# Batch 7's normalization factor through DRAM, batch 5's q transposed by DMA, and a new order, in a linear-attention and gated-FFN kernel

## The chip, the cores and the metric

The kernel runs on one core of a Trainium2 chip. The metric is the device time of one execution in microseconds (us). TensorE (PE; its weight loads are PEld) multiplies matrices into PSUM, VectorE (DVE) and ScalarE (ACT) work element by element, GpSimd (POOL) here issues the loads that cast from fp32 to bf16, and SyncE (SP) issues DMAs without a cast. Each engine runs its own instructions in program order and waits on semaphores for the others.

## What is computed

```python
def _attn_ref(q, k, v, g_norm):                    # q, k, v: (8, 8, 576, 64)
    kv = np.einsum('bhsd,bhse->bhde', k, v)
    out = np.einsum('bhsd,bhde->bhse', q, kv)
    rms = np.sqrt(np.mean(out * out, axis=-1, keepdims=True) + 1e-06)
    return (out / rms * g_norm).astype(np.float32)

def _moe_ref(x, w_in, conv_w, w_out):              # x: (8, 576, 512), d_ff 1024
    h = np.maximum(x @ w_in, 0.0)
    hp = ...                                       # h with one row of zeros at each end
    for k in range(3):
        conv_out += conv_w[k][None, None, :] * hp[:, k:k + S, :]
    gate = 1.0 / (1.0 + np.exp(-conv_out))
    return (h * gate @ w_out).astype(np.float32)
```

x is the attention's output with the heads side by side. The inputs are fp32; the products run in bf16.

## The kernel before

**Layout.** Between the two products everything is held transposed: features on the 128 partitions, the 576 positions of a batch along the free dimension. The 512 features of x are four tiles t of 128 (two heads each), the 1024 of h eight tiles f. Positions are halved into e = 0, 1 of 288 (HS) where a PSUM bank of 512 fp32 would be too small. Batches go in pairs p (0 to 3); x and h of a pair share a tile.

**The order is written out by hand.** ORDER (L66) is a list of tokens such as `sp.7.0@4,0`: the operation `sp` with arguments 7 and 0, and behind the @ the slots of ring buffers or PSUM banks that it takes, in turn. `:1` picks the other engine for operations that can run on ScalarE or VectorE. A loop (L732) calls the operations in this order, and L742 to L750 fix it on every engine. Between engines only data and buffers order the work, so a token's place matters against the tokens of its own engine.

**Stages of a batch b.**
- Loads: `Lq`, `Lk`, `Lv` (L299) through GpSimd's queue, one DMA of 590 KB in bf16 each (batch 1 in halves), into two slots a letter; `Li` and `Lo` load the weights. Batch 0 comes in `pre` (L215): q, k and v by pairs of heads through GpSimd's queue (L239), except the first k and v, which SP loads in fp32 into `stg` (L220) and `ca` (L326) casts on VectorE.
- `kv` (L356): k transposed times v, per head; `kvc`, or `kvn` with `ky` or `kx`, copy it to SBUF.
- q has to be transposed. Batches 0 to 4's way, `qt` or `qtp`, is TensorE (L378; for the batches in QP, 4 and 5, in the form of L386), and `qc` copies the result out of PSUM. For the batches in QD (6 and 7) `dq` (L434) has SP transpose q from SBUF to SBUF by DMA.
- q times kv: `ot` (L428, L429), or `oq` (L462) for the batches of QP and QD.
- `sq` (L491) squares on ScalarE, `oc` copies the product to `o32` in SBUF.
- The normalization. For batches 2 to 7, `ss` (L573) sums the squares of each head with the selector `sel`, so that a tile `ss` holds, for each t, rows of (batch in its group, e, head). NORM (L58) tells which batches share such a tile: group 3 is 6 and 7. `ln` (L582) takes the reciprocal root on ScalarE, `sl` (L589 to L592) splits the fp32 result into three bf16 parts on VectorE, `sp` (L601) spreads them over the 64 partitions of a head with a matmul against `spread`, which also adds the parts, and `mu` (L608) multiplies product, g_norm and factor on VectorE into xT. `ln` needs another table of ScalarE than the sigmoid (L211 loads tables).
- `hm` (L619): x times w_in, 8 matmuls a token; `re` (L625, L627) applies the relu into h.
- The convolution and the gate on five groups c (CONV, L63; groups 2 to 4 are pairs of batches): `ta` (L661, L662) the outer taps, `aa` (L668) and `ab` (L674) the sums, `sg` (L680) the sigmoid on ScalarE, `mg` (L686) the product with h.
- `om` (L696; `oh`, L711, for the last tile): h times w_out, by 128 positions m of pair p; `ea` or `eh` copies to a row tile, `st` or `sh` (L730, L725) stores it through SP.

**Fillers.** `unread.n` (L425) is n matmuls whose result nobody reads. 39 stand in the order of before, 10 of them ahead of the first q.

**Around the change.** SP's queue holds the two staged loads, then, from 63 us on, the stores, the four `dq` and four `kx` of batches 6 and 7. ScalarE's queue has the two small loads of g_norm and conv_w and the first table load at its head. qT, o32, row, k, v and the others are rings of slots by name. Which slots a load takes decides on whose last reader it waits.

Of the kernel before, what the change touches and what calls it, by code (L numbers as in the profile page):

```python
# [68 lines left out]
on.0.0@4 ot.0.1@2 qt0.0.2@6 nl.0.0@0 sq.0.1@1 unread.4@7 kv.0.2.1@7 on.0.1@4 qc0.0.2:1@1 al.x0@0 mu0.0.0 kvc.0.2.1.0
kvc.0.2.1.1:1 qt0.0.3@6 nl.0.1@1 ot.0.2@0 Li.0 unread.3@7 kv.0.3.1@7,4 mu0.0.1 sq.0.2@2 qc0.0.3:1 al.h0@0  # L70
kvc.0.3.1.0 on.0.2@2 kvc.0.3.1.1:1 ot.0.3@6 nl.0.2@2 sqh.0.3.0@3 Li.3 mu0.0.2 unread.3@5 onh.0.3.0@2 sqh.0.3.1
nlh.0.3.0@3 onh.0.3.1 Lq.1.2 nlh.0.3.1 qt.1.0@0 qc.1.0:1@2 Lv.1.2 unread.7@5 kv.1.0.2@0 muh.0.3.0 muh.0.3.1
kvc.1.0.2.0@1 kvc.1.0.2.1 unread.2@5 ot.1.1@0 sq.1.1@4 hm.0.0@6 on.1.1@2 hm.0.1@4 re.0.0 nl.1.1@4 ta.0.0@0 mu0.1.1
ot.1.0@6 hm.0.6@2 hm.0.7@0 Lk.1.2 re.0.1 sq.1.0@5 re.0.6 ta.0.1 aa.0.0 ta.0.6@1 on.1.0@2 qt.1.1@4 re.0.7 kv.1.2.2@0
nl.1.0@5 ab.0.0 qc.1.1@3 kvc.1.2.2.0 Li.1 kvc.1.2.2.1 ta.0.7 mu0.1.0 Lv.2.0@0 unread.3@1 ot.1.2@0 Li.2 Lk.2.0@0
ot.1.3@4 sq.1.2@6 unread.2@2 on.1.2@6 Lq.2.0@0 Lk.3.0@1 aa.0.3 sq.1.3@7 on.1.3@2 ab.0.3 nl.1.2@6 hm.0.3@6 nl.1.3@7
mu0.1.2 sg.0.0 hm.0.2@0 sg.0.1 re.0.2 mu0.1.3 hm.1.2@4 hm.0.5@2 sg.0.7 sg.0.6 re.0.3:1 Lv.3.0@1 pl mg.0.0 hm.1.3@6
hm.1.0@0 ta.0.2@0 al.x1@1 re.0.5 re.1.2 ta.0.3 re.1.0 mg.0.3 kv.2.0.4@2 aa.0.1 re.1.3 al.h1@1 ab.0.1 hm.1.1@4
ta.1.2@1 ta.1.3 hm.0.4@6 hm.1.7@0 aa.1.1 kvc.2.0.4.0@0 sg.0.2 sg.0.3 kvc.2.0.4.1 re.1.1 re.0.4 re.1.7 Lq.3.0@1
qt.2.0@2 qt.2.1@4 mg.0.1 hm.1.5@6 ab.1.1 ta.0.4@0 qc.2.0@4 Lo.0 sg.1.2 sg.1.3 ot.2.0@2 ta.0.5 hm.1.4@0 re.1.5  # L80
sq.2.0@0 qc.2.1@0 oc.2.0@0 mg.1.1 ot.2.2@4 ot.2.1@6 re.1.4:1 sq.2.2@1 kv.3.0.4@2 aa.0.2 oc.2.2@1 ot.2.3@0
kvc.3.0.4.0:1@1 sq.2.1@2 ab.0.2 ta.1.0@1 oc.2.1 sq.2.3@3 hm.1.6@4 ss.2@3 qt.3.1@6 re.1.6:1 sg.0.5 qt.3.0@4 oc.2.3
kvc.3.0.4.1:1 sg.0.4 qc.3.1@1 qc.3.0@2 ta.1.1 ln.8@0 unread.1@0 ot.3.3@6 unread.1@0 ot.3.0@4 Lo.1 ot.3.2@0 sq.3.0@4
mg.0.2 oc.3.0@2 Lq.4.0@0 aa.1.0 om.0.0.0@2 ta.1.4@0 sl.8@0 ta.1.5 ab.1.0 aa.1.2 sq.3.2@5 om.0.1.0@3 oc.3.2@3
om.0.2.0@4 sq.3.3@6 ot.3.1@0 om.0.0.4 oc.3.3 om.0.2.4 sq.3.1@7 oc.3.1 sp.2.0@6,0 ea.0.0@0 ss.3@5 ea.0.2@1 om.0.3.0@2
mu.2.0.0 ln.1@0 mu.2.0.1 sp.2.1@4,6 Lv.4.0@0 om.0.3.4 Lk.4.0@0 mu.2.1.0 qtp.4.0@0 sg.1.0 mu.2.1.1 sl.1@0 hm.2.6@4
qc.4.0:1@3 hm.2.2@6 re.2.6 ea.0.3@2 ab.1.2 re.2.2 sp.3.0@4,0 sg.1.4 sg.1.1 om.0.1.4 mu.3.0.1 mu.3.0.0 kv.4.0.4@2
sg.1.5 kvn.4.0.4 sp.3.1@0,6 ky.4.0.4.0 ea.0.1@3 hm.2.5@4 ky.4.0.4.1 re.2.5 mu.3.1.1 mu.3.1.0 hm.2.4@6 Lq.5.0@1
# [692 lines left out]
```

## Time and profile before

| what | us |
|---|---|
| median of 3 runs (180.3 to 180.98) | 180.41 |
| the profiled execution | 180.37 |
| its span, first to last instruction | 178.6 |
| first staged load issued (SP) | 0.75 |
| first matmul on data | 5.85 |
| last TensorE instruction | 174.45 |
| first table load of ScalarE | 2.37 |
| transposes of batch 6 and 7 by DMA issued | 86.3, 92.3, 94.6, 97.0 |

The granted TensorE clock is 0.996 of full speed over the span. The span starts with the first instruction and ends with the last; 1.8 us of the time lie around it. Busy time of TensorE includes the draining of a pipelined matmul: the cost of one in a row is the distance from its start to the next one's. The same holds, less strongly, for ScalarE and VectorE, whose instructions overlap by about 0.1 us. The DMA share is that of the 16 engines; above 1 it counts overlapping packets.

### The profile page before, as it was taken

The numbers are of one execution on the slowest core, as the hardware profiler recorded it, in microseconds if no ns is written. First come the engines' busy times: TensorE is split into PE (matmuls) and PEld (weight loads), VectorE is DVE, ScalarE is ACT, GpSimd is POOL, SyncE is SP. The second block draws the span as 40 slices with busy tenths as digits, with TensorE's granted clock in tenths as the row PEclk, the third lists the DMA queues.
The fourth block names the chain that finished last, engine by engine and source line by source line (L and its number), as shares of the span: only waits on it lengthen the run. The fifth ranks groups of instructions, "written<-read, shape, count | busy, mean of one in ns | idle before, by whom it ended". The sixth has DMA issues, their size and how long they took to land.

```text
span 178.6 us, 4103 instructions
## 1 busy us (share of the span) xinstructions
PE 170.6 (96%) x1680; PEld 101.0 (57%) x1680; DVE 140.4 (79%) x238; ACT 149.2 (84%) x235; POOL 30.6 (17%) x54
## 2 busy tenths in 40 slices
PE   6999997999999999999999999999999999999990
PEld 2434664787545677737657774344678744445450
DVE  5544199799999899999999999968999999930000
ACT  2479679999999999999999999999789986853341
POOL 7985528005320210600000000000000000000000
PEclk9999999999999999999999999999999999999998
DMA  5999999999999999999939700420340003046574
GB/s 150 193 183 197 200 201 202 204 205 204 205 204 204 204 207 251 175 188 193 153 99 228 207 4 0 165 101 32 136 158 0 4 0 117 0 185 225 186 259 149
DMA packets 32619, 27.58 MB, mean 154 GB/s; under 512 B 6080, under 2 KB 28120, under 8 KB 32600
## 3 DMA queue, kind: packets, MB, share of 16 engines
q0 software_dynamic: 21760, 15.96, 59.0%
q1 hardware_dynamic: 10800, 11.34, 20.3%
q8 instruction: 13, 0.21, 0.5%
q14 instruction: 6, 0.05, 0.1%
q10 hardware_dynamic: 40, 0.01, 0.0%
HBM read 32.52 MB, written 9.44 MB: 235 GB/s over the span
## 4 chain that ended last, share of the span: by engine, by line
PE 76%; ACT 10%; DVE 4%; DMA 3%; POOL 3%; issue 2%; POOLq 0%; ACTq 0%
PE bank L696 35%; PE bank L619 27%; ACT taps L680 3%; DMA q_sb<-in_q_dram 3%; ACT h L625 3%; PE bank L356 3%; PE bank L425 2%; PE bank L601 2%; PE bank L462 2%; PE bank L429 1%; PE bank L386 1%; POOL q_sb L239 1%; PE bank L573 1%; ACT o L339 1%; PE bank L711 1%
## 5 line engine op out<-in xcount | busy, mean ns | idle before, releaser
L619 PE MATMUL bank<-xT,w_in_sb 128*128 128x288 bf16 x512 | 66.3, 286 | 0.6 <-ACT root L540 0.6
L696 PE MATMUL bank<-w_out_sb,h 128*128 128x512 bf16 x280 | 64.3, 380 | 0.0
L619 PEld LDWEIGHTS <-w_in_sb 128*128 128x128 bf16 x512 | 49.1, 98 | 15.2 <-issue 1.7
L696 PEld LDWEIGHTS <-h 128*128 128x128 bf16 x280 | 26.1, 98 | 30.5 <-issue 1.2
L680 ACT ACTIVATE taps<-taps,cwn 128x1152 bf16<-128x1152 bf16 (+1 forms) x40 | 41.4, 1087 | 2.1 <-DVE taps L674 2.0
L625 ACT ACTIVATE h<-bank 128x576 bf16<-128x576 f32 x61 | 38.5, 680 | 2.4 <-PE bank L619 1.7
L339 ACT ACTIVATE row<-bank 128x512 f32<-128x512 f32 (+1 forms) x37 | 21.6, 604 | 11.6 <-PE bank L696 8.5
L686 DVE TENSOR_TENSOR h<-h,taps 128x2304 bf16<-128x2304 bf16 (+1 forms) x20 | 22.1, 1114 | 2.5 <-ACT taps L680 2.4
L668 DVE TENSOR_TENSOR taps<-taps 128x2304 bf16<-128x2304 bf16 (+1 forms) x20 | 22.3, 1119 | 0.4
L674 DVE TENSOR_TENSOR taps<-taps,h 128x2304 bf16<-128x2304 bf16 (+1 forms) x20 | 22.3, 1113 | 0.2
L661 DVE TENSOR_SCALAR taps<-h,cwn 128x1152 bf16<-128x1152 bf16 (+1 forms) x40 | 18.6, 465 | 4.3 <-ACT h L625 4.3
L491 ACT ACTIVATE sq<-bank 128x576 bf16<-128x576 f32 x28 | 19.1, 712 | 1.0 <-PE bank L429 1.0
L608 DVE SCALAR_TENSOR_TENSOR xT<-o,cw,bank 128x576 bf16<-128x576 f32 x24 | 18.2, 810 | 1.6 <-PE bank L601 1.5
L662 DVE TENSOR_SCALAR taps<-h,cwn 128x1152 bf16<-128x1152 bf16 (+1 forms) x40 | 18.2, 455 | 0.0
L339 ACT ACTIVATE o<-bank 128x576 f32<-128x576 f32 x24 | 16.9, 725 | 0.0
L425 PE MATMUL bank<-fill 128*128 128x512 bf16 x39 | 12.4, 445 | 1.5 <-DVE fill L226 1.5
L211 ACT ACT_TABLE_LOAD x8 | 10.3, 1283 | 2.5 <-issue 2.4
L356 PEld LDWEIGHTS <-k_sb 96*64 96x64 bf16 x384 | 7.3, 113 | 3.3 <-issue 3.1
L299 POOL DMA_DIRECT2D q_sb<-in_q_dram x8 | 6.0, 752 | 16.1 <-PE bank L378 14.3
L356 PE MATMUL bank<-v_sb,k_sb 96*64 96x64 bf16 x384 | 8.3, 197 | 0.2
L299 POOL DMA_DIRECT2D k_sb<-in_k_dram x8 | 6.1, 765 | 13.7 <-PE bank L356 13.1
L299 POOL DMA_DIRECT2D v_sb<-in_v_dram x8 | 6.0, 751 | 12.6 <-PE bank L601 11.4
(83 smaller groups left out, 122.8 us busy)
## 6 DMA issues: line engine op xcount, KB each, us to landing
out_dram<-row SPq DMA_DIRECT2D x35, 256.0 KB, 2.5
v_sb<-in_v_dram POOLq DMA_DIRECT2D x6, 576.0 KB, 13.8
k_sb<-in_k_dram POOLq DMA_DIRECT2D x6, 576.0 KB, 14.1
q_sb<-in_q_dram POOLq DMA_DIRECT2D x6, 576.0 KB, 14.3
w_in_sb<-in_moe_w_in_dram POOLq DMA_DIRECT2D x4, 256.0 KB, 10.8
w_out_sb<-in_moe_w_out_dram POOLq DMA_DIRECT2D x2, 512.0 KB, 19.4
q_sb<-in_q_dram POOLq DMA_DIRECT2D x4, 144.0 KB, 4.4
q_sb<-in_q_dram POOLq DMA_DIRECT2D x2, 288.0 KB, 8.2
```

Source lines behind the costliest of these rows:

```text
L339: nc.scalar.activation(to, fr, AX.Copy)
L356: nc.tensor.matmul(ps[i][i * D:(i + 1) * D, t - t0, :], k_sb[:, 2 * t + i, r * D:(r + 1) * D], v_sb[:, 2 * t + i, r * D:(r + 1) * D], star ...
L491: nc.scalar.activation(in_order(b, s), product(b, t), AX.Square)
L608: nc.vector.scalar_tensor_tensor(x_tile(b)[:, 2 * u:2 * u + 2, n], T["o32", b, u][:, :, n], g_sb, T["sp", b, e][u][:, :, :HS], op0=AL.mult ...
L619: nc.tensor.matmul(ps[:, e, :HS], w_in_sb[:, t, f * P:(f + 1) * P], x[:, t, e * HS:(e + 1) * HS], start=(t == 0), stop=(t == NT - 1))
L625: nc.scalar.activation(to, fr, AX.Relu)
L661: nc.vector.tensor_scalar_mul(tap[:, 0, f % 2, :n, 8:8 + S], h[:, f], cwn[:, 0, f:f + 1])
L668: nc.vector.tensor_add(tap[:, 1, :, :n, :S], tap[:, 0, :, :n, 7:7 + S], tap[:, 1, :, :n, 1:1 + S])
L674: nc.vector.tensor_add(y, y, h[:, 2 * j:2 * j + 2])
L680: nc.scalar.activation(y, y, AX.Sigmoid, scale=cwn[:, 1, f:f + 1])
L686: nc.vector.tensor_mul(h, h, T["tap", c, j][:, 1, :, :n, :S])
L696: nc.tensor.matmul(T["om", p, m], h[:, f, m * P:(m + 1) * P], w_out_sb[:, f, :], start=(f == 0), stop=(f == NF - 1))
```

## The change

- NORM gives batches 6 and 7 a group each (3 and 4): `ss.6` and `ss.7` write tiles of their own, and `ln` runs for each, five times in all. `sl` still runs four times: group 4 has none.
- Batch 7 (FD) gets its factor another way: `fw` stores the fp32 root (128 x 288) to DRAM through SP, `fr` reads it back in fp32 with two DMAs for each half e, each of them one row of every t to 64 partitions, into a slot of v; `mu` reads that tile where it read PSUM. `sp.7.0` and `sp.7.1` are gone.
- Batch 5 moves from QP to QD: `dq.5.0` and `dq.5.1` through SP where `qtp.5.0`, `qtp.5.1` and their copies `qc` were. On SP they stand ahead of the first store.
- Batch 0's first q joins k and v in `stg`: k and q through SP, v through ScalarE's queue ahead of its two small loads. `ca` casts q on VectorE, k and v on ScalarE. GpSimd's queue begins with the second q.
- The order is new throughout, and some choices of engine with it: `oc.2.2`, `kvn.4`, `kvn.6`, `ea.0.5` and one half of `kvc` for two pieces of batch 0 go to VectorE, the other half of the first to ScalarE; of `re`, 0.2 goes to VectorE, 0.3 and 1.6 to ScalarE. Fillers are 38, 9 of them ahead of the first data. Among the loads, those of batches 4 to 7 change places within a batch or two.

The diff, with the order cut to lines that hold the tokens named:

```diff
...
 AL = mybir.AluOpType
 PSUM = bass.MemoryType.PSUM
 
-NORM = {8: [2], 1: [3], 2: [4, 5], 3: [6, 7]}
+NORM = {8: [2], 1: [3], 2: [4, 5], 3: [6], 4: [7]}
 SPLIT = (0, 3)
-QD = (6, 7)
-QP = (4, 5)
+QD = (5, 6, 7)
+QP = (4,)
 QUAD = QD + QP
+FD = (7,)
 CONV = {0: (0, 1), 1: (1, 1), 2: (2, 2), 3: (4, 2), 4: (6, 2)}
 
 
 ORDER = """
-pre@0,0,0 pi unread.10@0 qt0.0.0@0 qc0.0.0:1@0 ps pn ca.k.0 ca.v.0 kv.0.0.1@1 kvc.0.0.1.0:1@0 kvc.0.0.1.1 Lq.1.0@1
...
-sq.4.2@2 oc.4.2@1 sq.4.3@3 hm.3.6@2 oc.4.3 re.3.6 sg.2.5 ky.5.0.4.0:1 qtp.5.1@6 al.x2@0 Lk.7.0@1 Lv.7.0@1 om.0.7.4
...
-qc.5.1@0 ta.2.6@1 sg.2.4 qtp.5.0@2 ky.5.0.4.1:1 qc.5.0@1 hm.2.7@6 hm.3.2@4 re.2.7 oq.5.2@2 ea.0.7@4 oq.5.3@6
...
-om.1.3.0@6 ea.1.6@1 om.1.1.0@7 ta.3.4@1 ta.3.5 aa.3.2 oc.7.3 ab.3.2 sl.3@0 sp.7.0@4,0 mu.7.0.0 om.1.0.0@2 mu.7.0.1
...
-ea.1.2@2 sp.6.1@2,0 om.1.8.0@6 mu.6.1.1 sg.3.5 re.5.6 ea.1.1@4 mu.6.1.0 ea.1.8@6 ta.3.6@0 sp.7.1@2,4 hm.4.7@0
...
-ea.3.7@5 st.3.4 st.3.7 oh.3.8.1 eh.3.8.1 sh.3.8.1
+pre@0,0,0 pn ca.k.0:1 ps pi ca.q.0 ca.v.0:1 unread.9@0 kv.0.0.1@0 kvc.0.0.1.0@0 qt0.0.0@1 kvc.0.0.1.1 ct@2 qt0.0.1@0
...
+al.h0@0 al.x0@0 al.x1@1 qc0.0.0:1@0 pg ot.0.0@2 kv.0.1.1@1 qc0.0.1:1 pc kvc.0.1.1.0:1 al.h1@1 Lq.1.0@1 kvc.0.1.1.1:1
...
+mu.3.1.0 oq.4.0@2 hm.2.4@0 sq.4.0@0 sg.1.4 oc.4.0@0 mu.3.1.1 hm.3.4@4 ta.1.6@1 re.2.4 dq.5.0@4 re.3.4 oq.4.2@2
...
+oq.4.1@4 Lk.5.0@1 sg.2.4 re.3.0 ta.2.6@1 dq.5.1@1 kv.5.0.4@6 ta.2.7 sq.4.1@3 hm.2.2@2 om.0.8.0@7 kvn.5.0.4:1 aa.2.3
...
+aa.2.1 st.0.0 ss.5 ln.2@0 ea.0.5:1@6 ab.2.1 ta.2.0@1 kv.6.0.4@2 oc.5.2@2 om.0.7.4 sl.2@0 Lq.7.0@0 Lq.6.0@1
...
+ss.7@1 oq.6.2@6 ta.3.4@0 hm.4.6@2 ln.4@0 om.1.6.0@1 sq.6.2@5 oc.6.2@1 re.4.6 ta.3.5 ea.1.5@4 oq.6.1@2 oq.6.3@6
...
+ea.1.8@2 sq.6.1@6 sq.6.3@7 oc.6.3 om.1.0.0@4 ss.6@0 oc.6.1 aa.3.2 hm.5.6@6 om.1.2.0@2 fw.4 ln.3@0 ea.1.0@1 ea.1.6@3
...
+re.5.6 fr.7.0@0 st.1.7 ab.3.2 sl.3@0 sp.6.0@6,0 mu.6.0.1 mu.6.0.0 om.1.1.0@4 mu.7.0.0 sp.6.1@6,0 st.0.4 mu.6.1.1
...
+mu.6.1.0 ea.1.4@7 mu.7.0.1 sg.3.0 om.1.3.0@5 sg.3.1 sg.3.5 fr.7.1@1 st.1.4 hm.4.7@0 st.1.0 al.h3@1 ea.1.2@0 mg.3.0
...
+hm.6.2@6 hm.6.5@2 mu.7.1.0 ea.1.1@6 re.4.7 ta.3.6@1 ea.1.3@5 re.6.2 sg.3.4 ta.3.7 mu.7.1.1 hm.6.0@4 hm.6.3@6 re.6.0
...
+eh.3.8.0@4 om.3.5.4 oh.3.8.1 ea.3.5@0 sh.3.8.0 eh.3.8.1 st.3.5 sh.3.8.1
 """
 
 
...
     def pre():
         for x in "qkv":
             qkv[x, 0] = ring(x, [PS, H, R * D], BF16, name=x + "_sb")
-        T["stg"] = work.tile([PS, 2, 2, R * D], FP32, name="stg", tag="h0", bufs=1)
-        for i, x in enumerate("kv"):
-            nc.sync.dma_start(out=T["stg"][:, i], in_=heads(x, 0, 0, 2))
+        T["stg"] = work.tile([PS, 3, 2, R * D], FP32, name="stg", tag="h0", bufs=1)
+        for i, x, queue in ((1, "k", nc.sync), (2, "v", nc.scalar), (0, "q", nc.sync)):
+            queue.dma_start(out=T["stg"][:, i], in_=heads(x, 0, 0, 2))
         nc.scalar.dma_start(
             out=cw_rows[NC:].rearrange("p (i d) -> p i d", i=2),
             in_=g_norm.unsqueeze(0).unsqueeze(0).to_broadcast([1, 2, D]))
...
         for i in range(2):
             nc.vector.memset(ones[i * D:(i + 1) * D, i * D:(i + 1) * D], 1.0)
         nc.vector.memset(kvbd[1], 0.0)
-        for n, (x, t) in enumerate([(x, t) for t in range(NT) for x in "qkv" if t or x == "q"]):
+        for n, (x, t) in enumerate([(x, t) for t in range(1, NT) for x in "qkv"]):
             if n == 2:
                 nc.gpsimd.affine_select(
                     out=ident, in_=ident, compare_op=AL.not_equal, fill=1.0,
...
 
     @op
     def ca(x, t):
-        nc.vector.tensor_copy(qkv[x, 0][:, 2 * t:2 * t + 2, :], T["stg"][:, "kv".index(x)])
+        copy(qkv[x, 0][:, 2 * t:2 * t + 2, :], T["stg"][:, "qkv".index(x)], pick[0] == 1)
 
     def last():
         return nc.cur_bb.bb.instructions[-1]
...
                 T["w", g][rows], start=True, stop=True, tile_position=(t * 32, 0))
 
     @op
+    def fw(g):
+        T["fac", g] = nc.dram_tensor(f"factor{g}", (NT, 32, HS), FP32).ap()
+        nc.sync.dma_start(out=T["fac", g].rearrange("t c n -> (t c) n"), in_=T["rs", g])
+
+    @op
+    def fr(b, e):
+        f = T["f", b, e] = ring("kv"[b % 2], [P, NT, HS], FP32, name="factor")
+        at = 4 * NORM[NG[b]].index(b) + 2 * e
+        for i in range(2):
+            nc.sync.dma_start(
+                out=f[i * D:(i + 1) * D],
+                in_=T["fac", NG[b]][:, at + i, :].unsqueeze(0).to_broadcast([D, NT, HS]))
+
+    @op
     def mu(b, e, u):
         n = slice(e * HS, (e + 1) * HS)
+        if b in FD:
+            nc.vector.scalar_tensor_tensor(
+                x_tile(b)[:, 2 * u:2 * u + 2, n], T["o32", b, u][:, :, n], g_sb, T["f", b, e][:, 2 * u:2 * u + 2, :],
+                op0=AL.mult, op1=AL.mult)
+            return
         nc.vector.scalar_tensor_tensor(
             x_tile(b)[:, 2 * u:2 * u + 2, n], T["o32", b, u][:, :, n], g_sb, T["sp", b, e][u][:, :, :HS],
             op0=AL.mult, op1=AL.mult)
```

More of the change, by code (lines that the diff above doesn't have):

```diff
@@ L69 @@
[L69 to L88, printed above, removed]
@@ new lines @@
+sp.2.0@0,6 ab.1.2 mu.2.0.0 ss.3@4 mu.2.0.1 ea.0.3@2 ln.1@0 om.0.1.0@5 sp.2.1@0,2 mu.2.1.0 om.0.1.4 mu.2.1.1
+qtp.4.0@6 sl.1@0 sg.1.0 qc.4.0:1@3 ea.0.1@3 hm.2.0@0 qtp.4.1@2 hm.2.7@6 re.2.0 qc.4.1@0 sp.3.0@4,0 mu.3.0.1 mu.3.0.0
+kv.4.0.4@2 sg.1.5 sg.1.1 Lv.5.0@1 hm.2.5@0 kvn.4.0.4:1 ky.4.0.4.0 re.2.7 mg.1.0 sp.3.1@4,6 ky.4.0.4.1 re.2.5
+mu.3.1.0 oq.4.0@2 hm.2.4@0 sq.4.0@0 sg.1.4 oc.4.0@0 mu.3.1.1 hm.3.4@4 ta.1.6@1 re.2.4 dq.5.0@4 re.3.4 oq.4.2@2
+ta.1.7 oq.4.3@6 mg.1.2 sq.4.2@1 aa.1.3 oc.4.2@1 hm.3.5@0 hm.2.6@4 hm.3.3@2 sq.4.3@2 re.3.5 oc.4.3 hm.2.3@0 ta.2.4@0
```

65 lines of the change are left out of this document (38 added, 27 removed).

## The prediction

> **What bounds the kernel now.** I read the busy shares first, then the chain that ended last, then busy time by stage, then the groups and landings that the change touches. First the page:
>
> ```profile
> span 178.6 us, 4103 instructions
> PE 170.6 (96%) x1680; PEld 101.0 (57%) x1680; DVE 140.4 (79%) x238; ACT 149.2 (84%) x235; POOL 30.6 (17%) x54
> ...
> DMA  5999999999999999999939700420340003046574
> GB/s 150 193 183 197 200 201 202 204 205 204 205 204 204 204 207 251 175 188 193 153 99 228 207 4 0 165 101 32 136 158 0 4 0 117 0 185 225 186 259 149
> ...
> PE 76%; ACT 10%; DVE 4%; DMA 3%; POOL 3%; issue 2%; POOLq 0%; ACTq 0%
> ```
>
> TensorE is the engine of the chain, and the DMA engines are full until slice 19 (85 us). The chain in order of time shows where each of the two rules:
>
> ```profile
> 6.39 5.57 DMA q_sb<-in_q_dram
> ...
> 48.00 0.22 PE bank L429
> 48.22 0.22 PE bank L425
> ...
> 51.86 0.22 PE bank L429
> 52.07 1.73 PE bank L696 x8
> 53.80 0.34 PE bank L601 x4
> 54.14 0.36 PE bank L573 x8
> 54.50 0.97 PE bank L696 x4
> ```
>
> From 48 us to 174.5 us it is TensorE alone, one product behind the other; before that it changes between loads, ScalarE, VectorE and TensorE. Busy time by stage (columns: us, then PE, PEld, DVE, ACT, POOL, granted clock, DMA share, GB/s):
>
> ```profile
> 12.00:43.00 31.00, 29.68 (x386) 19.72 (x387) 23.13 (x47) 27.23 (x49) 13.01 (x25) 1.00 1.34 201
> 60.00:80.00 20.00, 20.00 (x270) 13.33 (x269) 19.47 (x35) 19.91 (x35) 4.59 (x6) 1.00 1.26 206
> 80.00:100.00 20.00, 20.00 (x251) 12.87 (x251) 19.75 (x27) 19.91 (x31) 0.00 (x0) 1.00 0.97 173
> 100.00:120.00 20.00, 20.00 (x148) 10.74 (x147) 18.10 (x24) 19.95 (x32) 0.00 (x0) 1.00 0.22 80
> ```
>
> ScalarE and VectorE are nearly as full as TensorE, so whatever is taken from TensorE counts only while the other two keep up.
>
> **The sum is made on TensorE's queue.** I took every token's distance from its first matmul to the next token's first, in stretches without a wait: hm 0.98 us, om of 8 matmuls 1.73, kv of 48 0.88, qtp 0.512, ss 0.36, sp 0.233, oq 0.185. These add to 153.3 us for the order of before. The first real matmul starts at 5.85 us, the last ends at 174.45: 168.6 us, of which 153.3 are work, 8.4 are the 29 filler matmuls behind the start with what they waited, and 6.8 are losses (some 4 before 48 us, the rest steps of 0.1 us). After 174.45 come the last copy and store.
>
> **Taken from TensorE.** Batch 5's transposes (qtp.5.0 and qtp.5.1, 24 of the 48 matmuls of L386): 2 x 0.512 = 1.02 us. Batch 7's spreads (sp.7.0, sp.7.1, 8 of the 48 matmuls of L601): 2 x 0.233 = 0.47 us. Fillers behind the start stay 29. Both stood in the stretch in which TensorE alone makes the chain: -1.49 us.
>
> ```profile
> L601 PE MATMUL bank<-wparts,spread 32*128 32x288 bf16 x48 | 3.8, 291 | 0.0
> L386 PE MATMUL bank<-ident,q_sb 96*128 96x96 bf16 x48 | 2.7, 206 | 0.0
> ```
>
> **The head.** Three fp32 loads of 288 KB (k and q on SP, v on ScalarE's queue) stand where two were, and GpSimd's queue loses q's first 144 KB. The two loads of L220 landed at 0.75 + 3.2 = 3.95 and 1.21 + 3.8 = 5.0 us, 1.06 us apart; a third lands near 6.0. Then come its cast (0.55 us, the row of L326), the transposes 0.40, the copy 0.65: the first product starts near 7.8 instead of 7.50. On the DMA engines 288 KB at the 277 GB/s of the stretch 2 to 4 us cost 1.06 us, and the 147 KB taken from GpSimd's queue at 188 GB/s were 0.78: all later loads come 0.3 us later. Until 48 us the work follows them closely (q's last piece lands at 11.96 and its transposes start at 12.01), so I charge +0.3 us. Bounds: -0.65 (one GpSimd issue less, if that queue and not the engines paces) and +1.06 (a whole load more). The 0.3 is what the engines' occupancy gives, and they are full. ScalarE's issue of v comes before its two small loads and its table load; ScalarE sat idle 2.9 us there, which hides this and its two casts (0.8 us each, between its 0.65 us for 576 and 1.13 for 1152 elements). If that cover goes, kv.0.0.1 waits up to 0.8 us, and then the products behind it.
>
> **ScalarE and VectorE behind the head**, by the rows' means. ScalarE: + ln.4 0.53, + one re net 0.68, - oc.2.2 0.73, - two kvn 0.78, - ea.0.5 0.62, - one kvc net 0.22: -1.1 us; table loads stay 8 (ln.4 takes ln.3's). VectorE: - two copies qc.5 1.51, + what ScalarE gave up (oc 0.75, kvn 0.84, ea 0.70, kvc 0.22), - one re 0.75: +0.3 us. Batch 7's four mu read the factor from SBUF instead of PSUM; L608 (0.81 us) and L560 (0.81, its factor in SBUF) give 0. Between 43 and 143 us VectorE is busy 96.3 us of 100 and ScalarE 97.9, so both still fit into 98.5. Charged 0; bounds -0.3 to +1.5 (the whole saving lost).
>
> **Batch 5's transposes by DMA** now stand first on SP's queue, ahead of every store, and wait for q's load (11.83 MB into the stream: by the GB/s row near 60.5 us, landed near 62). Queued behind them is st.0.0; the first store of before was issued at 63.2, so nothing is held up.
>
> ```profile
> L434 SPq DMA_TRANSPOSE qT<-q_sb x4: 1312/1320/1658, 86.3 to 97.0; - x4
> ...
> DMA to landing us min/median/max: 3.4/3.6/3.8
> ```
>
> Those four ran when the loads were over or nearly so. Two now run among full engines. One takes 2 us of the engines (the stretch 93.5 to 95.5 is 1.12 busy with one). Batch 5's k and v come 1.18 MB behind q: 5.8 us at 204 GB/s, 67.8 us, and with both transposes served first 71.7 us. kv.5 stands near 72.6 us of the new order (70.64 before, 1.9 us more work ahead of it). Charged 0, margin 0.9 us. The other bound: a transpose has 1,150 packets by the DMA records, 72 an engine; if each waits for one packet of the loads (77 ns: 59.0% of 178.6 us on 16 engines over 21,760 packets), two take 2 x 72 x (77 + 27 ns) = 15 us (27: 2 us of 16 engines over 1,150) and land near 79; oq.5.2 comes near 81. [...]
>
> **Batch 7's factor through DRAM.** ss.7 starts near 112.5 us (60.1 us of TensorE work behind it). ScalarE then has oc.7.1 0.53, a table load 1.30, ln.4 0.50: 114.9. fw is a store like L730's (256 KB, 2.5 us): 117.4. SP waits for it, behind SP stand st.1.7, st.0.4 and fr.7.1. fr.7.0 is two loads of 288 KB as L220's: the second lands 4.26 us after the first's issue, 121.6. VectorE's turn for mu.7.0.0 comes behind sp.6.0 (8.4 us of TensorE work after ss.7 starts, 121.0), its 0.23 and two mu of 0.73: 122.8. Margin 1.2 us; charged 0. Behind mu.7.0.0 stand mu.6.1.*, and for those hm.6.2: TensorE has 4.67 us of work up to there, VectorE five mu, 3.65, so another 1.0 us is covered. fr.7.1 (+1.7 us of issues) has 1.5. The round trip is 6.8 us; bounds 5.6 (2.4 + 3.2) and 13.2 (twice the 6.6 us of L730's slowest landing). I take 6.8 because the DMA engines are 22% busy at 100 to 120 us.
>
> **The end.** Behind mg.4.3 the new order has 13.0 us of TensorE work against 15.6; mg.4.3 came at 157.2 us, so the tail gains slack, not time. The last stores keep their form.
>
> Sum: -1.49 + 0.3 = -1.2 us on the profiled execution's 180.37 us (span 178.6 and 1.8 around it): 179.2. The median of the runs, 180.41, is the same to 0.04. Differences under 0.5% (179.5 to 181.3) are no change that can be told.
>
> **Rivals.**
> *Another engine is the bound.* The saving turns into TensorE waits. For it: 19.91 and 19.75 of 20 us. Against it: TensorE shows no gap over 0.15 us from 55 us on. If VectorE rules, the time moves with its +0.3: 180.6. [...]
> *Batch 5 is late.* Transposes and st.0.0 (another 1 us of the engines) ahead of k's load: 72.7 against 72.6, and anything more is a wait before kv.5, one for one: with 1 to 3 us, 180.2 to 182.2. For it: the DMA share of 1.26 at 60 to 80 us. Against it: turn by turn the transposes, not k, would be the late ones, and they have more room.
> *The factor is late* (slower than before). Place: mu.7.0.0. It costs one for one beyond 1.2 + 1.0 us; beyond 3.4 us late, a round trip over 10.2 us, the kernel is slower than before. At 13.2 us: 6.4 late, 4.2 lost, 183.4. For it: two DMAs and two waits in a row on SP. Against it: idle DMA engines.
> *The order gains more.* The landing of a load plus the TensorE work behind its first use is a floor for the end. The highest floor is 58.9 + 111.9 = 170.8 us before (batch 4's k) and 45.35 + 124.1 = 169.5 after (batch 3's v, with the 0.3 in it), 1.3 lower; the 0.3 would then cost nothing, and if the losses before 48 us, 4 us, also shrink by 1, the time is 177.9. Against it: ScalarE paces much of that stretch (28 to 43 us of the chain).
> That the first q by SyncE starts nothing earlier is no rival: the sum has it later.
>
> **Chances.** Forecast 0.55 (its own range 178.3 to 179.9: 0.47 under 179.5, 0.08 within), more gained 0.08, another engine 0.12 (0.09 within, 0.03 slower), batch 5 late 0.12 (0.07 within, 0.05 slower), factor late 0.13 (slower). Faster 0.47 + 0.08 = 0.55, same 0.08 + 0.09 + 0.07 = 0.24, slower 0.03 + 0.05 + 0.13 = 0.21. The range 178.0 to 181.8 reaches from just above the gained case over both cases in the middle; it leaves out half of the gained case, the worst of batch 5 and most of the late factor, near 0.2 together.
>
> **What would show it.** No L386 row for 24 of 48, L601 x40, six L434 with the first two landing by 72 us; no TensorE wait on q, k or v after 55 us; no VectorE wait before L608's successor for batch 7; the last matmul near 173.3 us. Wrong if TensorE's chain between 55 us and the end has waits above 1 us, or if the work until 48 us starts over 1 us later.

## The result and the profile after

The changed kernel takes 182.55 us in the median (182.35 to 183.41) against 180.38 us: 1.0119 times as long, 95% interval 1.0084 to 1.0153. It is slower, beyond the 181.8 us at which the predicted range ended. (In this document a time is the median of all executions of a kernel, while a ratio and its interval leave out the few that are over 1.5% above the fastest of the same kernel, so the two need not divide.) The profiled execution took 182.35 us, 2.0 more than the one of before. Its page:

```profile
span 180.5 us, 4055 instructions
PE 170.6 (94%) x1647; PEld 100.6 (56%) x1647; DVE 140.6 (78%) x239; ACT 150.8 (84%) x234; POOL 29.7 (16%) x53
...
PEclk9969999999999999999999999999999999999998
DMA  5999999999999999999975992039560000608654
...
PE 73%; DVE 15%; ACT 5%; DMA 3%; issue 1%; SPq 0%; DVEq 0%
```

TensorE runs fewer matmuls in the same busy time, the third slice of PEclk (the granted clock, 9.0 to 13.5 us) reads 6 where all later ones but the last read 9, and VectorE's share of the chain went from 4 to 15%. The chain in order of time names the places:

```profile
1.21 5.32 DMA stg<-in_q_dram
...
46.87 1.33 DVE h L706 x2
50.48 2.59 PE bank L716 x12
...
62.26 1.54 DVE xT L628 x2
63.80 0.34 DVE kvn L342
64.17 0.38 ACT kvx L340
64.56 0.65 ACT h L645
...
66.33 2.12 PE bank L639 x16
...
91.78 1.55 DVE xT L628 x2
93.38 0.95 PE bank L357 x48
```

It begins with the first q, as before, now by SyncE, and from 50 us it is no longer TensorE alone: VectorE's `mu` cuts in at 62 and 92 us, and at 62 us VectorE's and ScalarE's copies and a relu follow it. The first product of x (`hm`) starts at 21.05 us in this chain and at 19.77 in that of before, 1.28 us later; TensorE's last instruction ends 2.4 us later. So in these two executions about half of the delay is there by 21 us. Busy time by stage, the same stretches as before (columns as there):

```profile
12.00:43.00 31.00, 30.00 (x394) 18.98 (x393) 23.19 (x49) 26.82 (x47) 12.68 (x25) 1.00 1.34 202
60.00:80.00 20.00, 18.66 (x246) 13.71 (x244) 18.50 (x32) 18.77 (x32) 3.82 (x5) 1.00 1.38 167
80.00:100.00 20.00, 19.64 (x237) 11.24 (x235) 19.69 (x30) 18.63 (x28) 0.77 (x1) 1.00 0.99 158
100.00:120.00 20.00, 20.00 (x155) 11.68 (x154) 18.75 (x23) 19.89 (x32) 0.00 (x0) 1.00 0.51 130
```

At 60 to 100 us all three engines have more pauses than before: TensorE 1.7 us where it had none, ScalarE 2.6 where it had 0.2, VectorE 1.8 where it had 0.8. The waits of ScalarE there, and then TensorE's (columns: us in total, times, longest); in before the lists of ScalarE and of TensorE's matmuls for this stretch are empty:

```profile
ACT kvx L340 <- DVE kvn L342: 1.2, 1, 1.2
ACT h L645 <- PE bank L639: 0.8, 1, 0.8
ACT taps L700 <- DVE taps L694: 0.4, 1, 0.4
```

```profile
PE bank L602 <- ACT h L645: 0.8, 1, 0.8
PE bank L639 <- ACT h L645: 0.4, 1, 0.4
PE bank L357 <- DVE xT L628: 0.3, 1, 0.3
```

The first of them is the join at 63 to 66 us: `kvn.4`, given to VectorE, stands behind two `mu`; ScalarE waits for it with `ky.4.0.4.0`, the relus re.2.7 and re.2.5 stand behind that, and they hold the PSUM banks that `sp.3.1` and `hm.2.4` need. From 100 us on the profile shows no wait of a matmul in either kernel; the last TensorE instruction ends at 176.85 instead of 174.45 us.

What the change removed is gone, batch 5's transposes (which before were TensorE's, like those of batches 0 to 4) included, and no matmul waited for its two transfers. The row of a DMA gives how long its issue held SP (minimum, median and maximum in ns) and the starts of the first and the last issue:

```profile
L602 PE MATMUL bank<-wparts,spread 32*128 32x288 bf16 x40 | 3.3, 291 | 0.8 <-ACT h L645 0.8
...
L387 PE MATMUL bank<-ident,q_sb 96*128 96x96 bf16 x24 | 1.4, 206 | 0.0
```

```profile
L435 SPq DMA_TRANSPOSE qT<-q_sb x6: 1295/2046/5802, 62.0 to 103.0; - x6
...
DMA to landing us min/median/max: 3.5/8.3/15.8
```

### The profile page after: what moved, and what is told of

The parts are those of the page before. It is cut to its first block, busy times and chain, and to the rows that moved or that the text cites. A ratio compares the mean times of both kernels' runs of the same rounds, so it can differ in the third digit from the quotient of the medians.

```text
span 180.5 us, 4055 instructions
## 1 busy us (share of the span) xinstructions
PE 170.6 (94%) x1647; PEld 100.6 (56%) x1647; DVE 140.6 (78%) x239; ACT 150.8 (84%) x234; POOL 29.7 (16%) x53
## 4 chain that ended last, share of the span: by engine, by line
PE 73%; DVE 15%; ACT 5%; DMA 3%; issue 1%; SPq 0%; DVEq 0%
PE bank L716 34%; PE bank L639 26%; DMA stg<-in_q_dram 3%; PE bank L357 2%; DVE taps L681 2%; PE bank L426 2%; DVE h L706 2%; DVE taps L682 2%; DVE xT L628 2%; PE bank L463 2%; PE bank L430 2%; DVE taps L694 2%; DVE qT L342 2%; DVE taps L688 2%; DVE xT L561 1%; ACT root L541 1%
## 5 line engine op out<-in xcount | busy, mean ns | idle before, releaser
L716 PEld LDWEIGHTS <-h 128*128 128x128 bf16 x280 | 26.6, 98 | 30.5 <-issue 0.7
L340 ACT ACTIVATE row<-bank 128x512 f32<-128x512 f32 (+1 forms) x36 | 20.4, 590 | 11.1 <-PE bank L716 9.0
L492 ACT ACTIVATE sq<-bank 128x576 bf16<-128x576 f32 x28 | 18.1, 670 | 1.3 <-PE bank L430 1.3
L628 DVE SCALAR_TENSOR_TENSOR xT<-o,cw,bank 128x576 bf16<-128x576 f32 x20 | 15.4, 810 | 2.0 <-PE bank L602 1.7
L340 ACT ACTIVATE o<-bank 128x576 f32<-128x576 f32 x23 | 15.1, 682 | 0.0
L561 DVE SCALAR_TENSOR_TENSOR xT<-bank,cw,root 128x576 bf16<-128x576 f32 x7 | 5.6, 812 | 3.0 <-ACT root L541 3.0
## 6 DMA issues: line engine op xcount, KB each, us to landing
k_sb<-in_k_dram POOLq DMA_DIRECT2D x6, 576.0 KB, 15.8
```

Source lines behind the costliest of these rows:

```text
L340: nc.scalar.activation(to, fr, AX.Copy)
L628: nc.vector.scalar_tensor_tensor(x_tile(b)[:, 2 * u:2 * u + 2, n], T["o32", b, u][:, :, n], g_sb, T["sp", b, e][u][:, :, :HS], op0=AL.mult ...
L716: nc.tensor.matmul(T["om", p, m], h[:, f, m * P:(m + 1) * P], w_out_sb[:, f, :], start=(f == 0), stop=(f == NF - 1))
```

## Experiments on the head

All ratios are to the kernel before, timed beside each kernel; its median lay between 180.48 and 180.64 us.

**a_headq, the old head.** q's first piece goes back to GpSimd's queue, k and v to SP and their casts to VectorE, with ten fillers ahead, in the changed kernel.

```diff
...
-        for i, x, queue in ((1, "k", nc.sync), (2, "v", nc.scalar), (0, "q", nc.sync)):
-            queue.dma_start(out=T["stg"][:, i], in_=heads(x, 0, 0, 2))
+        for i, x in enumerate("kv"):
+            nc.sync.dma_start(out=T["stg"][:, i], in_=heads(x, 0, 0, 2))
...
```

> The changed kernel with only its head undone: the first q comes by GpSimd's queue into bf16 again, k and v by SP with VectorE's casts, ten fillers ahead; all behind the first product is the changed order. Theory (the head is paid in full: first product at 8.40 us instead of 7.50, and from 8.5 to 11.9 us a granted clock of 0.5 behind the idle TensorE): first product back near 7.5, clock 1.0 throughout, and the end 1.0 to 1.3 us earlier, 181.2 to 181.6. Rival (the loss sits in the new order on VectorE from 22 to 66 us, which paces whatever comes before): under 0.3 us gained, 182.3 or more.

Measured: 181.01 us, 1.0025 (1.001 to 1.0039). The new head costs 1.5 us; behind it the change loses the whole saving and 0.5 us more. The clock is not steady in this kernel either: eight of its twelve executions (180.64 to 181.07 us) have a mean granted clock of 0.998 or more, four (181.56 to 183.39 us) one of 0.981 to 0.990. In the changed kernel all four are at 0.981 to 0.989.

**a_fill, the new head with 15 fillers for 9.**

```diff
-... unread.9@0 ...
+... unread.15@0 ...
```

> The changed kernel with fifteen fillers instead of nine ahead of the first product, to last until the first data at 6.7 us. Theory (the clock fell to 0.5 from 8.5 to 11.9 us because TensorE was idle from 5.4 to 6.7): granted clock 1.0 from 5 us on, matmuls of 512 columns back from 0.43 to 0.22 us there, and 0.5 to 0.9 us off the end, 181.7 to 182.1. Rival (the dip costs nothing, since ScalarE's chain of batch 0 paces those products): clock 1.0 but 182.4 to 182.6.

Measured: 181.67 us, 1.006 (1.004 to 1.0081), 0.9 us less than the changed kernel: that part of the 1.5 us is TensorE's clock. Windows of the changed kernel (column 3 is TensorE's busy time, the third from the end its granted clock), then of a_fill:

```profile
5.08:8.49 3.41, 1.72 (x40) 1.31 (x39) 1.13 (x4) 2.80 (x6) 2.77 (x5) 1.00 1.29 205
8.49:11.90 3.41, 3.41 (x32) 1.52 (x32) 1.83 (x7) 1.97 (x4) 3.32 (x6) 0.50 1.31 199
```

```profile
4.77:8.18 3.41, 3.07 (x45) 1.76 (x44) 1.03 (x3) 2.49 (x5) 2.99 (x6) 1.00 1.27 207
8.18:11.60 3.42, 2.79 (x48) 1.58 (x48) 2.38 (x9) 2.92 (x6) 3.25 (x6) 1.00 1.31 199
```

Nine fillers end at 5.35 us, and q lands at 6.53. TensorE was busy for 1.72 of the 3.41 us from 5.08 to 8.49 us, and from 8.49 to 11.90 its granted clock was 0.50. In a_fill, with TensorE busy for 3.07 of the 3.41 us from 4.77 on, the clock kept 1.00; behind the next 3.42 us there, with 2.79 busy, it kept 1.00 too.

**b_head and b_headfill, the new head in the kernel before**, with 9 and with 15 fillers.

```diff
-pre@0,0,0 pi unread.10@0 qt0.0.0@0 qc0.0.0:1@0 ps pn ca.k.0 ca.v.0 kv.0.0.1@1 kvc.0.0.1.0:1@0 kvc.0.0.1.1 Lq.1.0@1
+pre@0,0,0 pn ca.k.0:1 ps pi ca.q.0 ca.v.0:1 unread.9@0 kv.0.0.1@1 kvc.0.0.1.0@0 qt0.0.0@0 kvc.0.0.1.1 qc0.0.0:1@0 Lq.1.0@1
```

> The kernel before with only the new head: q staged in fp32 with k and v, casts of k and v on ScalarE and of q on VectorE, nine fillers. Theory (the head costs its late start and the clock): 1.0 to 1.4 us slower than before, 181.4 to 181.8, first product near 8.4 us, a stretch of clock 0.5. Rival (the loads set the pace up to 45 us and hide it): within 0.3 us of before, 180.2 to 180.7.

> The kernel before with the changed head (first q by SyncE), now with 15 matmuls on unread data ahead of the first work where b_head had 9. Theory (TensorE's clock): in b_head's profile the 128x512 products took 0.61 us until 12.3 us and 0.38 us from 14.7 us on, and the clock's record begins only at 13.98 us; its three slow runs paid about 3 us for that, its one run of 180.88 us did not. With fillers up to 6.4 us the record begins below 6 us in every run, no run is above 181.8 us, and the median is 180.7 to 181.2 us: the loads' new order itself costs 0.2 to 0.7 us. Rival (the later landing of q and of the second tiles): the median stays at 182.5 us or more although the products take 0.38 us from 8.4 us on.

Measured: b_head 183.13 us, 1.0113 (1.005 to 1.0176), three times of 182.86 to 183.45 and one of 180.88; b_headfill 181.14 us, 1.0019 (0.9991 to 1.0047). The timeline of TensorE in b_head, at 8.75 and at 14.72 us, has the same product at two speeds:

```profile
8.75 0.61 PE L429 MATMUL bank<-qT,kvbd 128*128 128x512 bf16 x1
...
14.72 0.38 PE L429 MATMUL bank<-sq,ones 128*128 128x512 bf16 x1
```

In that execution the record of the granted clock begins only at 13.98 us; the first product of x comes at 22.77 us instead of 19.77, and the last product of all 3.0 us late as well. In b_headfill's profiled execution, at full clock, the first product of x is 0.45 us late and the last one 0.47. So what is late in the head is late at the end. Without the clock the new head is worth some 0.5 us in the medians and in these profiles, though the interval of b_headfill's ratio does not tell it from nothing. (Stretches ahead of that record read 1.00 in a table by stage, 10.57 to 13.98 us too; the instruction's own time, 0.61 against 0.38 us, tells.)

**a_headqf, the old head with three fillers more** behind the first product.

```diff
-... ot.0.0@2 kv.0.1.1@1 ...
+... ot.0.0@2 unread.3@4 kv.0.1.1@1 ...
```

> The changed kernel with the old head, as a_headq, and three matmuls on unread data behind the first product, which fill the idle stretch 8.9 to 9.5 us of a_headq's profile. Theory (a_headq's runs with a dip of the clock, 181.56 to 183.39 us, come from that stretch): no run has a dip, all lie between 180.5 and 181.2 us, median 180.8 us. Rival (the dip has another cause, or the fillers delay the first tiles by what they save): runs above 181.4 us remain, median 181.0 us or more.

Measured: 182.21 us, 1.01 (1.0038 to 1.0163), worse than a_headq. Two of four executions (182.21 and 184.25 us) still had a mean clock below 0.992, so the rival holds: the fillers did not end the falls of the clock. The other two lie at 181.92 and 182.20 us with their clock kept. The first of them is the profiled one, and it shows a wait of TensorE at 18 us for batch 1's v:

```profile
PE bank L357 <- DMA v_sb<-in_v_dram: 0.8, 1, 0.8
```

Before has no such wait in its profile, but b_noq5's profiled execution has one of 0.9 us. In the profiled executions this load landed between 17.45 us (a_headq) and 18.86 us (a_headqf), with 17.82 in before and 18.50 in b_noq5. That such waits, beside falls of the clock (executions of the kernel before at 181.67 to 181.93 us have a mean clock of 0.986 or 0.987), make the spread of these kernels is likely; only the profiled executions can show it.

## Experiments on the order and the saving

**a_kvn4 and a_join, the join at 63 to 66 us.** a_kvn4 is the changed kernel with `kvn.4` back on ScalarE. a_join is a_headqf with that, and two relus moved ahead.

```diff
-... kvn.4.0.4:1 ...
+... kvn.4.0.4 ...
```

```diff
-kv.4.0.4@2 sg.1.5 sg.1.1 Lv.5.0@1 hm.2.5@0 kvn.4.0.4:1 ky.4.0.4.0 re.2.7 mg.1.0 sp.3.1@4,6 ky.4.0.4.1 re.2.5
-mu.3.1.0 oq.4.0@2 hm.2.4@0 sq.4.0@0 sg.1.4 ...
+kv.4.0.4@2 sg.1.5 re.2.7 Lv.5.0@1 hm.2.5@0 kvn.4.0.4 ky.4.0.4.0 ky.4.0.4.1 sp.3.1@4,6 re.2.5
+mu.3.1.0 oq.4.0@2 sg.1.1 hm.2.4@0 sq.4.0@0 mg.1.0 sg.1.4 ...
```

> The changed kernel with one token other: batch 4's copy kvn.4 on ScalarE, as before the change, instead of VectorE. Theory (kvn.4 stands on VectorE behind two mu of batch 3; ScalarE's copies to kvx wait for it, the relu re.2.7 stands behind them, and TensorE waits 1.7 us for its banks between sp.3.1 and hm.2.4): the two waits, 1.2 and 0.5 us, go, and the time falls by 1.3 to 1.7 us to 180.9 to 181.3. Rival (VectorE is simply late there and TensorE's wait moves on to the next product): under 0.4 us.

> a_headqf, and around 62 to 67 us: batch 4's state copied by ScalarE as before, the relu re.2.7 ahead of it, re.2.5 behind both swapped copies, one sigmoid (sg.1.1) and its product behind them. Theory (the new order puts two relus, which hold PSUM banks, behind copies that wait for VectorE; TensorE loses 1.8 us there): the two waits of 0.77 and 0.36 us vanish and the time falls by 0.9 to 1.8 us against a_headqf, to 179.0 to 179.9 us, below the kernel before. Rival (ScalarE and VectorE are full until 70 us, so a wait taken out comes back at the next product): a gain of 0.4 us or less.

Measured: a_kvn4 182.18 us, 1.009 (1.0061 to 1.0119), 0.4 us less than the changed kernel, whose executions overlap with these (181.77 to 182.77 against 182.35 to 183.41); a_join 180.76 us, 1.0013 (0.9981 to 1.0046), equal to before. Against a_headqf a_join gains 1.4 us, but most of that is the head's spread: against a_headq, whose head is the same but for the three fillers, it is 0.25 us, less than either interval can tell. TensorE's waits at 60 to 70 us in a_join:

```profile
PE bank L639 <- DVE xT L628: 0.4, 1, 0.4
PE bank L639 <- ACT h L645: 0.3, 1, 0.3
```

The wait of 0.8 us is gone, and another engine's came in its place. So the join's wait is the order's, and taking it out gains little: a wait taken out came back at the next product, as the rival had it.

**b_dq5, batch 5's transposes by DMA alone**, in the old order.

```diff
-QD = (6, 7)
-QP = (4, 5)
+QD = (5, 6, 7)
+QP = (4,)
...
-... qtp.5.1@6 ... qc.5.1@0 ... qtp.5.0@2 ... qc.5.0@1 ...
+... dq.5.1@0 ... dq.5.0@1 ...
```

> The kernel before with one part of the change alone: batch 5's two sets of 12 transposes leave TensorE and their two copies leave ScalarE and VectorE; the two DMA transposes stand in the old order's place. Theory (the parts are worth what TensorE saves, the head and the order gave it back): 2 x 0.512 us less on TensorE, so 179.3 to 179.9 us against 180.5. Rival 1 (the transposes land late, near 80 us, where the first use was at 75 and the second at 78.7): TensorE waits 1 to 3 us there and the time is 180.5 to 182.5 us. Rival 2 (ScalarE and VectorE set the pace, so TensorE's saving is idle time): 180.3 to 180.7 us.

Measured: 181.23 us, 1.0001 (0.9972 to 1.003), in two groups, four of 179.77 to 180.36 and five of 181.13 to 181.71 us, and one execution of 184.76. The profiled execution (181.71 us) is of the upper group; it loses at the late transposes and behind them. The rows of the transposed q in its trace, and who waited for it (us in total, times):

```profile
L434 SPq DMA_TRANSPOSE qT<-q_sb x6: 1247/1322/6067, 63.2 to 99.8; - x6
...
  POOL q_sb L299: 5.8, 1
  PEld L462: 0.9, 1
```

GpSimd's load of batch 7's q waits 5.8 us for the transposes to give the buffer back; dq.6.0 is issued at 90.3 instead of 86.3 us, and oq.6.1 then waits 1.1 us for a `kx` queued behind it on SP. With the changed kernel's places the first transposes are issued 1.1 us earlier, and no product waits for them; GpSimd's load still does, 0.9 us in the changed kernel and 3.6 in a_join. Two of the lower group (179.77 and 179.87 us) lie below all 25 executions of the kernel before beside it (180.16 and up). The mean of the four is 180.08 us against a median of 180.58 before, so where the transposes come in time this part may be worth up to half a microsecond; no profile of that group was taken.

**b_noq5, the saving with no DMA in its place.** Batch 5's products read batch 4's transposed q.

```diff
-... qtp.5.1@6 ... qc.5.1@0 ... qtp.5.0@2 ... qc.5.0@1 ...
+...
...
-                    T["qx", b, t // 2][half, at:at + HS], start=True, stop=True, tile_position=(e * D, i * D))
+                    T["qx", 4 if b == 5 else b, t // 2][half, at:at + HS], start=True, stop=True, tile_position=(e * D, i * D))
```

> The kernel before; batch 5's q is neither transposed nor copied: its products read batch 4's transposed q (so batch 5's output is another). It takes 2 x 0.512 us off TensorE, 1.13 us off ScalarE and 0.75 us off VectorE at 72 to 75 us, and adds no DMA. Theory (the part is worth what the most loaded engine saves, and b_dq5's slower runs lost it to the late transposes and the loads behind them): 179.2 to 179.8 us, no second group of runs above 181 us. Rival (the engines are bound elsewhere, so even the free saving comes to nothing): 180.3 to 180.7 us.

Measured: 180.55 us, 1.0015 (0.9994 to 1.0036). The rival holds: 1.02 us taken from TensorE gains nothing that can be told (the interval allows 0.1 us). (Both copies are VectorE's, so the kernel also spares it 1.5 us and ScalarE nothing; the expectation had one of them on ScalarE.) This profiled execution (181.02 us) is 0.6 us late from the wait for batch 1's v on. VectorE's timeline in it (in brackets the pause ahead of an instruction and what ended it), and a wait of TensorE that the kernel before does not have:

```profile
74.34 0.81 DVE L661 TENSOR_SCALAR taps<-h,cwn 128x1152 bf16<-128x1152 bf16 x1 [0.36 <-ACT h L625]
75.07 0.84 DVE L662 TENSOR_SCALAR taps<-h,cwn 128x1152 bf16<-128x1152 bf16 x1
75.92 0.42 DVE L341 CAST kvx<-bank 64x256 bf16<-64x256 f32 x1
76.62 1.36 DVE L686 TENSOR_TENSOR h<-h,taps 128x2304 bf16<-128x2304 bf16 x1 [0.27 <-ACT taps L680]
```

```profile
PE bank L462 <- ACT h L625: 0.5, 1, 0.5
```

Where its two copies were, VectorE now waits for ScalarE, and mg.2.2 (L686) starts right behind the sigmoid, 0.55 us later than in before (76.07 us there, sigmoids from 73.45 to 75.98), by as much as the whole execution is late. In before ScalarE has no pause above 0.15 us from 28.3 to 126.2 us, and VectorE none above 0.16 from 61.6 to 109.1.

**b_act, b_pe, b_dve: more work on one engine at a time** in the kernel before, at 69 to 82 us.

```diff
+    def xa():
+        nc.scalar.activation(junk[:, 0], fill, AX.Square)
...
+    def xd():
+        nc.vector.tensor_tensor(junk[:, 1], fill, fill, op=AL.add)
...
-re.2.3 ... re.3.6 ... re.3.2
+re.2.3 xa ... re.3.6 xa ... re.3.2 xa
...
-hm.2.3@2 ... hm.3.6@2 ... hm.3.2@4 ... hm.3.1@4
+hm.2.3+2@2 ... hm.3.6+2@2 ... hm.3.2+2@4 ... hm.3.1+2@4
```

> The kernel before with three more ScalarE instructions (128x512 bf16, some 0.5 us each, nobody waits for their result) behind the relus re.2.3, re.3.6 and re.3.2, 69 to 76 us. Theory (ScalarE is a second bound: before has no idle ScalarE from 28 to 113 us): 1.2 to 1.6 us more, 181.8 to 182.2 us. Rival (TensorE alone sets the end): 0.4 us more or less.

> The kernel before with two matmuls on unread data ahead of each of hm.2.3, hm.3.6, hm.3.2 and hm.3.1 (69 to 82 us), 8 x 0.21 = 1.7 us. Theory (TensorE and ScalarE are both full there, each costs its own work): 1.3 to 1.8 us more, 181.9 to 182.4 us. Rival (ScalarE alone sets the pace there, TensorE has slack): 0.5 us more or less.

> The kernel before with six more VectorE instructions (128x512 bf16 sums that nobody reads, some 0.3 us each), two at each of b_act's three places. Theory (VectorE too has 0.1 us of idle time or less between 62 and 87 us): 1 to 2 us more. Rival (VectorE has slack that the order hides): 0.5 us more or less.

Measured: b_act 181.99 us, 1.0108 (1.0064 to 1.0152); b_pe 182.48 us, 1.0116 (1.0082 to 1.0151); b_dve 183.27 us, 1.0167 (1.0139 to 1.0195). Against 180.48 us these are 1.5, 2.0 and 2.8 us. From each start to the next, ScalarE's three take 0.52 us (1.6 in all; each lasts 0.76, overlapping its neighbour), TensorE's eight 0.21 (1.7) and VectorE's six 0.42 (2.5). So added work costs its whole length, within intervals of 0.5 to 0.8 us to either side, on whichever of the three engines it lands.

**b_nosq, b_noq5sq, b_nosq4, b_noq5sq4: less work on ScalarE**, after 79 us (batch 5's squares) or before 73 us (batch 4's), alone and with b_noq5. The left-out squares take their neighbours' place:

```diff
+    def su(b, t, o):
+        T["sq", b, t] = T["sq", b, o]
+        T["sqi", b, t] = T["sqi", b, o]
...
-sq.5.3@5 ... sq.5.1@7
+su.5.3.2 ... su.5.1.0
```

> The kernel before; two of batch 5's four squares on ScalarE are left out (the sum of squares of the tiles 5.1 and 5.3 reads those of 5.0 and 5.2, so batch 5's factors are others). It takes 2 x 0.53 = 1.06 us off ScalarE near 79 to 82 us and nothing off TensorE or VectorE. Theory (ScalarE, never idle from 28 to 126 us in the profile of before, sets the pace there): 0.6 to 1.1 us less, 179.4 to 179.9 us against 180.5. Rival (all three engines bind each other, so less work on one alone gains nothing, as b_noq5 showed for TensorE): 180.3 to 180.7 us.

> b_noq5 and b_nosq together: 1.02 us less on TensorE, 1.06 us less on ScalarE, 1.5 us less on VectorE. Theory (ScalarE sets the pace): as b_nosq within 0.3 us. Rival (all three bind): 0.7 to 1.1 us less than the kernel before, where each part alone gains nothing.

> As b_nosq, but the two squares left out are batch 4's (tiles 4.1 and 4.3; its factors are others): 1.06 us less on ScalarE between 66 and 73 us, where b_nosq took the same off between 79 and 82 us. Theory (ScalarE and VectorE tie: in before neither has more than 0.15 us of idle time from 62 to 109 us, and TensorE's work fits between): no change, 180.3 to 180.8 us. Rival (up to the product mg.2.2 at 76 us ScalarE alone sets the pace): 0.5 to 1.0 us less.

> b_noq5 and b_nosq4 together: before 76 us ScalarE has 1.06 us less, VectorE 1.5 us and TensorE 1.02 us. Theory (ScalarE and VectorE tie): with both relieved ahead of the same point the time falls by 0.6 to 1.1 us, to 179.4 to 180.0 us, although b_noq5 alone gained nothing. Rival (a fourth thing, the DMA loads or the chain of batch to batch, holds all three): 180.3 us or more.

Measured: b_nosq 180.64 us, 1.0003 (0.9982 to 1.0024); b_noq5sq 180.51 us, 0.998 (0.9952 to 1.0009); b_nosq4 180.13 us, 0.9982 (0.9956 to 1.0008); b_noq5sq4 180.14 us, 0.9975 (0.9959 to 0.9991). Only the last is told from no change, by 0.4 us; it leaves work out and is no kernel to use. ScalarE's waits at 78 to 90 us in b_nosq:

```profile
ACT h L630 <- PE bank L624: 0.9, 3, 0.4
```

Most of the 1.06 us comes back there as waits for TensorE's products. Ahead of 76 us the engines meet at mg.2.2: in before VectorE reaches it at 76.07 us without a pause, and the sigmoid that it needs ends at 75.98. With VectorE relieved (b_noq5) it waits for the sigmoid. With ScalarE relieved (b_nosq4) VectorE again comes to it without a pause, at 75.80 us, and ScalarE has stood 0.34 us for a product of TensorE at 72.45. From there VectorE has no pause until 109. A saving of 1 to 1.5 us on each of the three ahead of 76 us is worth 0.4; on ScalarE alone, on TensorE and VectorE alone, or behind 76 us on ScalarE, nothing that can be told from none. Which link holds the other 0.6 us was not separated.

**b_pool and b_poolonly, relief by GpSimd.** Two of the gate's products go to GpSimd, with a third buffer for the taps; in b_pool four relus also go from ScalarE to VectorE.

```diff
-name=f"taps{i}") for i in range(2)]
+name=f"taps{i}") for i in range(3)]
...
-ta.2.4@0 ... ta.2.2@0 ... mg.2.2 ... mg.2.1 ... re.3.2 ... re.3.0 ... re.4.2 ... re.5.0
+ta.2.4@2 ... ta.2.2@2 ... mp.2.2 ... mp.2.1 ... re.3.2:1 ... re.3.0:1 ... re.4.2:1 ... re.5.0:1
...
+    def mp(c, j):
...
+        nc.gpsimd.tensor_mul(h, h, T["tap", c, j][:, 1, :, :n, :S])
```

> A version meant to be faster, with the reference's result: in the kernel before, GpSimd takes two products of the gate (mg.2.2 and mg.2.1, 1.35 us each on VectorE, first read near 107 us) with a third buffer for the taps, and VectorE takes four relus (re.3.2, re.3.0, re.4.2, re.5.0) from ScalarE. ScalarE has 4 x 0.53 = 2.1 us less, VectorE as much as before. Theory (ScalarE sets the pace until 126 us): 1.0 to 2.1 us less, 178.4 to 179.5 us. Rival (GpSimd's products slow VectorE's instructions beside them, or VectorE's own chain binds): 180 us or more.

> b_pool without the four relus moved: VectorE has 2.7 us less, ScalarE and TensorE as before. Theory (ScalarE sets the pace): 180.2 to 180.7 us, no change. Rival (VectorE sets it): 1 to 2.5 us less.

Measured: 186.72 us, 1.0323 (1.0262 to 1.0383), and 186.16 us, 1.0222 (1.0136 to 1.0307). Both theories miss the size, and the direction. GpSimd's product, then VectorE's instruction of the same time, in b_poolonly:

```profile
76.12 4.54 POOL L692 TENSOR_TENSOR h<-h,taps 128x2304 bf16<-128x2304 bf16 x1 [0.47 <-issue]
```

```profile
76.56 4.43 DVE L661 TENSOR_SCALAR taps<-h,cwn 128x1152 bf16<-128x1152 bf16 x1 [0.40 <-ACT h L625]
80.91 0.51 DVE L662 TENSOR_SCALAR taps<-h,cwn 128x1152 bf16<-128x1152 bf16 x1
```

GpSimd needs 4.54 us for what takes VectorE 1.35, and an instruction of VectorE that takes 0.51 us lasts until 0.3 us after GpSimd is done. Part of the loss is TensorE's clock again. In b_poolonly's profiled execution (mean clock 0.976) TensorE then waits 2.1 us for VectorE's `sl`; it is busy for 1.30 us of the stretch 86.55 to 89.96 us, and from 89.96 to 96.79 the clock is 0.50. The one execution that kept its clock (mean 0.997) took 183.41 us, so some 3 us of the loss are left without it. No version with the reference's result beats the kernel before beyond its measurement; a_join equals it.

## Why the prediction was wrong, step by step

The forecast of 179.2 us is 3.35 us below the measured 182.55. Of these 1.49 are the saving that did not come, 1.24 the head (182.55 - 181.01 = 1.54 where 0.3 was charged), 0.47 the new order (a_headq, 181.01, over its neighbour's 180.54); the 0.15 that are left are that neighbour's, 180.54 against 180.38. The line between the saving and the order is reckoned: a_headq shows that the two together are 0.47 us slower than before, b_noq5 that 1.02 us of the 1.49 were worth nothing in the old order. The 0.47 us of the spreads were not tried alone, and which places of the new order cost the rest stays open but for the join.

- **The bound: the step that failed first.** "From 48 us to 174.5 us it is TensorE alone" was read from the chain, which follows one engine as long as that engine does not pause. ScalarE and VectorE did not pause either. The prediction wrote the condition down ("counts only while the other two keep up") and then answered it with a sum over 100 us. "Both stood in the stretch in which TensorE alone makes the chain: -1.49 us" has the right size of the work (24 matmuls fewer in L387's row, 8 in L602's) and the wrong worth: b_noq5 measures 0.0 for 1.02 of it.
- **"Both still fit into 98.5 ... Charged 0."** The bound "+1.5 (the whole saving lost)" is what happened. A sum of 97.9 us that fits into 98.5 says nothing of the order within it; in the new order ScalarE waited 2.4 us at 60 to 100 us.
- **The head, +0.3.** Direction right, size wrong, and above its upper bound of 1.06. q landed at 6.53 us, not near 6.0; the first product started at 8.40 us, not 7.8. A term was missing: the half clock of 8.49 to 11.90 us, 0.9 us by a_fill. The reason given for the 0.3, that all later loads come 0.3 us later, was wrong too: by the packet records batch 1's v had its last packet at 16.63 us against 16.65 and landed at 18.03 against 17.82, and batch 5's q landed at 61.94 us against 62.14, earlier than before. What came later was the first product.
- **Batch 5 by DMA: the charge of 0 was right, its first reason was not.** The two were to land by 71.7 us, before or with k; they landed at 73.67 and 79.81. The other bound, an estimate in which every packet of a transpose waits for one of the loads', gave 15 us and near 79; the longest landing took 15.8, which does not show that the packets take turns. TensorE did not wait for them, and kv.5 came at 76.0 us instead of 72.6 with its k landed since 68.96. In b_dq5, with the old order's places, the same transposes held a product up.
- **The factor: right.** fw was issued at 117.45 us (forecast 114.9) and landed in 1.8 us, the readings in 4.8 to 6.5. The first half's round trip took 8.0 us instead of 6.8; mu.7.0.0 came at 126.75 us, 1.3 us behind it, without a wait, near the forecast margin of 1.2 because VectorE's turn came later too.
- **The rivals.** "Another engine is the bound", at 180.6 us, is the mechanism of the lost saving, and had 0.12; its 180.6 us has neither the head nor the order's waits. By it TensorE's 1.49 us would be worth nothing, and b_noq5 shows that for 1.02 of them. But b_nosq took 1.06 us from ScalarE, the fullest of the others (84% busy on the page of before), and gained nothing either (1.0003). No rival had the clock. The two signs named as proving it wrong both came: TensorE's waits of 0.8 + 0.4 + 0.3 us, and qt.1.0 at 17.12 instead of 15.84 us. Of the signs that it was right, the rows of the removed work came; the landing by 72 us and a last matmul near 173.3 us (176.85) did not.
